# Sixteen instead of twenty-eight filling products of zeros on TensorE in the front of an attention and expert kernel

## The chip, the cores and the metric

The kernel runs on one core of a Trainium2 chip. The metric is the device time of one execution in microseconds (us); lower is better. A core has five engines that run side by side: PE (TensorE, whose loading of the stationary operand is shown apart as PEld), DVE (VectorE), ACT (ScalarE), POOL (GpSimd) and SP (SyncE, which here issues the DMAs).

## The reference, cut to what matters

A windowed attention with block summaries, for 4 batches of 8 heads, 768 positions and 64 features a head, and behind it a gated two-layer network on the 4 x 768 x 512 result.

```
scores_l = scale * q @ k.T           # kept where |i - j| < 16
scores_s = scale * q @ k_sum.T       # k_sum: maximum of each 32 keys; + log(32)
a = softmax([scores_l masked, scores_s])
x = a @ [v, v_sum]                   # v_sum: mean of each 32 values
xk, xr = mixes of x with x one position earlier (mu_k, mu_r)
out = sigmoid(xr @ w_r) * ((max(xk @ w_k, 0))**2 @ w_v)
```

## The kernel before, in words

A head pair fills the 128 partitions, so a batch has four sets (pairs), and each set is worked in two halves of 384 positions, which the code calls units. A unit is a row of steps on different engines: 24 small score products (L559, PE, into the banks `sc`), masking with a running minimum (L585, DVE), the exponential (L589, ACT), the inverse of the sums (L595 and L596, DVE), the scaling (L601, POOL), and for the first batch a transpose on PE (L608) whose result ACT copies out (L614); then 24 value products (L656). Before the first score of a set, DVE takes block maxima of the keys (L466 to L474) and copies them into the key tile `kt` (L478). For the first batch PE makes the block means of the values (L490, then L509 behind an ACT copy to the tile `sp` on L508); ACT copies them to `vm` (L511), and they are spread into the value tile `vx` (L515 or a DMA). The result of the attention goes to `vx` as well (L671), and is mixed (L682 on ACT or POOL, L688 on DVE) for the gate products (L730). The layers behind it are the products on L757 and L784, and for the last batch a seven-product scheme (L929, L1020). Weights come as 512 KB loads into three tiles `st`, are turned from 64-bit words into floats by ACT (L411) and DVE (L414, L416), and kept.

The order on every engine is fixed when the program is built: each step is an `op` with an engine, an assumed length and a due time, and `schedule()` places them one after the other by its own model of the engines, the DMA and the buffers. Steps without a buffer or with an unfinished input wait in lists; the earliest start wins, and among equals the earliest due time.

The front holds filling products too. `warm()` adds an op named "warm": one product of a 128 x 128 tile of zeros with itself (`zero_sb`, written once by POOL on L1066) into a free PSUM bank, which nothing reads. In the trace each shows as two matmul records and two weight loads of L440, so 28 of them are 56 records. `WARM` is how many are on offer. The planner takes one only where PE would otherwise stand idle for more than 300 ns by its own model and a bank is free, and none after a certain time or once the bank `pt` is given up:

```
    for _ in range(WARM):
        warm()
...
                if fill and (pick is None or pick[2] > fill[0] + GAP):
                    fill[1].place = spare[0][1]
                    pick = None, fill[1], fill[0]
```

With 260 on offer, 28 were taken, all in the first 20 us.

Of the kernel before, what the change touches and what calls it, by code (L numbers as in the profile page):

```python
# [65 lines left out]
PERIOD = 52000  # L66
STEP = 4800
SLACK = 400
WARM = 260
WARM_END = 110000  # L70
GAP = 300
COLD = 5000
# [236 lines left out]
def tile_kernel(ctx: ExitStack, tc: tile.TileContext, q, k, vT, v, consts, w_k, w_v, w_r, out):  # L309
# [129 lines left out]
    def warm():  # L439
        o = op("PE", "warm", 1.0e8, lambda: nc.tensor.matmul(  # L440
            o.place.tile(F32)[:, 512 - P:512], zero_sb, zero_sb, start=True, stop=True), reads=ZERO)
# [627 lines left out]
    for t in pools["y"]:  # L1069
        op("POOL", "tiny", None, lambda t=t: nc.gpsimd.memset(  # L1070
            t.tile(F32).rearrange("p (i c) -> p i c", c=P)[:, :, NK:P], 0.0))
    for _ in range(WARM):
        warm()
# [129 lines left out]
```

## Time and profile before

| what | before |
|---|---|
| median of 3 runs | 418.27 us (417.93 to 418.51) |
| the profiled execution, its own time | 418.56 us |
| its span, first to last instruction | 416.5 us |
| PE busy | 409.1 us (98%) |
| DVE, ACT, POOL busy | 344.8, 286.8, 125.9 us |
| records of L440 (filling products) | 56, between 1.0 and 20 us |

The span is 2.06 us shorter than the execution that it comes from. A row of the timeline gives the start in the span, the busy time of the merged stretch, engine, line, operation, tiles (written <- read), shapes and count; in brackets stands how long the engine was idle ahead of it, and what ended that. Matmul ends are modelled and take in the draining, so neighbouring rows overlap a little. The column PEclk is the granted TensorE clock as a share of full speed.

### The profile page before, as it was taken

To read this page: it belongs to the slowest core of one execution; us is meant where nothing else is said; L and a number is where in the kernel's file an instruction comes from. 1 tells how busy PE (TensorE), PEld (TensorE's weight loads), DVE (VectorE), ACT (ScalarE), POOL (GpSimd) and SP (SyncE) were. 2 spreads that over 40 slices of the span, in tenths; PEclk is the share of its full clock that TensorE was granted. 3 is DMA by queue.
4 is the path that set the end of the run, shared out by engine and by line. 5 is a ranking of instruction groups with operands and counts; after the bars stand their busy time and mean duration, and the time that the engine had idled before them with its cause. 6 is when DMAs were issued, how large, how long until landed. Compare 5 with 4: busy or idle time off the path is not lost.

```text
span 416.5 us, 9788 instructions
## 1 busy us (share of the span) xinstructions
PE 409.1 (98%) x3353; PEld 348.1 (84%) x3353; DVE 344.8 (83%) x1053; ACT 286.8 (69%) x815; POOL 125.9 (30%) x255
## 2 busy tenths in 40 slices
PE   8899999999999999999999999999999999999996
PEld 7654557788888888988888888988889899999996
DVE  3889999999998799889798778569386698878993
ACT  2889999899874599547674559466595675669710
POOL 0472565534660043502252000422433030104100
PEclk9999999999999999999999999999999999999999
DMA  8996679678878577777635454487855325230012
GB/s 295 407 296 216 222 257 318 235 251 235 240 210 264 173 248 196 230 267 247 215 120 159 158 183 172 133 297 200 252 150 143 103 75 146 59 113 15 0 59 94
DMA packets 48193, 79.68 MB, mean 191 GB/s; under 512 B 6736, under 2 KB 28176, under 8 KB 48144
## 3 DMA queue, kind: packets, MB, share of 16 engines
q1 hardware_dynamic: 48000, 78.78, 58.7%
q8 instruction: 26, 0.43, 0.4%
q10 hardware_dynamic: 144, 0.28, 0.3%
q14 instruction: 23, 0.19, 0.1%
HBM read 58.68 MB, written 20.07 MB: 189 GB/s over the span
## 4 chain that ended last, share of the span: by engine, by line
PE 83%; DMA 6%; DVE 5%; ACT 5%; issue 1%; SPq 1%; DVEq 0%; ACTq 0%
PE bank L784 24%; PE bank L757 23%; PE bank L929 14%; PE bank L656 5%; PE bank L1020 4%; PE bank L559 3%; PE bank L717 3%; PE bank L718 3%; PE bank L719 3%; DMA st<-in_w_r 2%; ACT y L589 2%; DMA st<-in_w_k 2%; DMA qt<-in_q 1%; DVE st L626 1%; DVE y L585 1%
## 5 line engine op out<-in xcount | busy, mean ns | idle before, releaser
L601 POOL TENSOR_SCALAR y<-y,rc 128x120 f32<-128x120 f32 x192 | 94.4, 510 | 130.5 <-DVE mn L585 49.2
L757 PE MATMUL bank<-xs,w 128*128 128x384 f32 x556 | 111.7, 349 | 0.0
L757 PEld LDWEIGHTS bank<-xs,w 128*128 128x128 f32 x556 | 98.1, 188 | 8.5 <-issue 1.0
L589 ACT ACTIVATE y<-y,mn 128x120 f32<-128x120 f32 x192 | 73.4, 384 | 15.3 <-DVE mn L585 15.1
L784 PE MATMUL bank<-w,kh 128*128 128x512 f32 x258 | 69.5, 397 | 0.4 <-DVE kh L770 0.4
L764 ACT ACTIVATE r<-bank 128x384 f32<-128x384 f32 x48 | 23.4, 488 | 51.0 <-PE bank L757 50.5
L784 PEld LDWEIGHTS bank<-w,kh 128*128 128x128 f32 x258 | 47.2, 188 | 9.4 <-DVE kh L770 0.7
L585 DVE CUSTOM_DVE_ANT_0 y<-bank,consts_sb 128x120 f32<-128x120 f32 x192 | 41.9, 273 | 0.1
L784 PE MATMUL bank<-w,kl 128*128 128x512 f32 x129 | 39.3, 397 | 0.0
L589 ACT ACTIVATION_READ_ACCUMULATOR y<-y,mn 128x1 f32 x192 | 36.2, 189 | 0.0
L656 PEld LDWEIGHTS bank<-pts,vx 120*64 120x64 f32 x768 | 24.0, 138 | 8.3 <-issue 7.1
L929 PE MATMUL bank<-xs,w 128*128 128x384 f32 x126 | 30.8, 337 | 0.0
L626 DVE STREAM_TRANSPOSE st<-y 128x384 f32<-128x384 f32 x48 | 27.1, 567 | 3.4 <-POOL y L601 2.8
L770 DVE CAST kh<-r 128x384 fp32r<-128x384 f32 x26 | 9.6, 370 | 23.0 <-ACT r L766 23.0
L784 PEld LDWEIGHTS bank<-w,kl 128*128 128x128 f32 x129 | 23.7, 188 | 5.6 <-issue 0.2
L685 POOL TENSOR_SCALAR xa<-vx,om_sb 128x384 f32<-128x384 f32 x11 | 8.7, 793 | 60.4 <-DVE xs L699 60.4
L656 PE MATMUL bank<-pts,vx 120*64 120x64 f32 x768 | 26.8, 224 | 0.0
L559 PEld LDWEIGHTS bank<-kt,qt 64*64 64x64 f32 x768 | 20.1, 133 | 7.9 <-issue 3.4
L559 PE MATMUL bank<-kt,qt 64*64 64x120 f32 x768 | 24.9, 268 | 1.7 <-DVE kt L478 1.1
L772 DVE TENSOR_TENSOR kl<-r,kh 128x384 fp32r<-128x384 f32 x43 | 24.1, 559 | 2.7 <-ACT kh L771 1.1
L766 ACT ACTIVATE r<-r 128x384 f32<-128x384 f32 x48 | 25.2, 525 | 0.7
L717 PE MATMUL bank<-w,xs 128*128 128x512 f32 x60 | 23.7, 395 | 0.0
(374 smaller groups left out, 824.2 us busy)
## 6 DMA issues: line engine op xcount, KB each, us to landing
vx<-in_v SPq DMA_DIRECT2D x32, 384.0 KB
far<-st SPq DMA_DIRECT2D x96, 96.0 KB
pts<-far SPq DMA_DIRECT2D x24, 384.0 KB
kt<-in_k SPq DMA_DIRECT2D x15, 544.0 KB
qt<-in_q SPq DMA_DIRECT2D x32, 192.0 KB
st<-in_vT SPq DMA_DIRECT2D x12, 384.0 KB
out<-z SPq DMA_DIRECT2D x18, 256.0 KB
st<-in_w_k SPq DMA_DIRECT2D x8, 512.0 KB
```

The lines of the kernel that those rows point to most:

```text
L559: nc.tensor.matmul(cells(to[h])[cs, i, 0:NK], t.t[hs, n * QW:(n + 1) * QW], kt.t[hs, w * KB:w * KB + NK], start=True, stop=True)
L585: op("DVE", "mask", None, lambda h=h, i=i, var=var: nc.vector.tensor_tensor_reduce(out=cells(y[h])[:, i, 0:NK], in0=cells(spot[h])[:, i, 0 ...
L589: op("ACT", "exp", None, lambda h=h, i=i: nc.scalar.activation(cells(y[h])[:, i, 0:NK], cells(y[h])[:, i, 0:NK], AF.Exp, bias=mn[h].t[:, i ...
L601: op("POOL", "norm", None, lambda h=h, i=i: nc.gpsimd.tensor_scalar(out=cells(y[h])[:, i, 0:NK], in0=cells(y[h])[:, i, 0:NK], scalar1=rc.t ...
L626: op("DVE", "flip", due - (FIRST_AHEAD if b == 1 else AHEAD) + 8000 + 600 * h, lambda h=h: nc.vector.transpose(out=turned()[:, :, h], in_= ...
L656: nc.tensor.matmul(av.t[hs, w * QW:(w + 1) * QW], windows(vw)[:, w, hs], weights_of(pts)[0:NK, 2 * c:2 * c + 2, h, i], start=True, stop=True)
L717: nc.tensor.matmul(ps.t, xh.t[:, ts], h, start=(p == 0), stop=False)
L757: nc.tensor.matmul(ps.t[:, 0:HT], w.t[:, p * P:(p + 1) * P], x[p][s].t, start=(n == 0), stop=(n == len(terms) * NPAIR - 1))
L766: op("ACT", "square", None, lambda: nc.scalar.activation(r.t, r.t, AF.Square), reads=[(r, 0)], writes=[(r, 0)])
L772: op("DVE", "sub", None, lambda: nc.vector.tensor_tensor(out=kl.t, in0=r.t, in1=kh.t.bitcast(F32), op=ALU.subtract), reads=[(r, 0), (kh, 0 ...
L784: nc.tensor.matmul(acc[t].t, a.t[:, t * P:(t + 1) * P], v.bitcast(F32) if single else v, start=start, stop=stop)
L929: nc.tensor.matmul(bank.t[:, 0:HT], pair[w].t[:, col:col + P], a[k][s].t, start=(first and n == 0), stop=(n == 3 * nk - 1), skip_group_che ...
```

## The change

One constant: the number of filling products on offer.

```
-WARM = 260
+WARM = 16
```

The planner takes all sixteen, at the first places where the old one took fillers, and has none left for the later places. The first place, eleven fillers ahead of the first score, is as before. The next place is PE between the first and the second set's scores (L559; `kt`, `qt` are keys and queries, `bank` a PSUM bank; the `x` at the end counts products, a filler being one). This is the difference there:

```order
 L559 MATMUL bank_0_158<-kt_0_110,qt_0_124 64x120 x2
 L559 MATMUL bank_0_161<-kt_0_110,qt_0_124 64x120 x2
-L440 MATMUL bank_0_122<-zero_sb 128x128 x10
+L440 MATMUL bank_0_122<-zero_sb 128x128 x5
 L559 MATMUL bank_0_158<-kt_0_127,qt_0_131 64x120 x2
 L559 MATMUL bank_0_161<-kt_0_127,qt_0_131 64x120 x2
```

Ten fillers have become five; nothing else stands elsewhere.

Then PE makes the first set's block means (L490), the second product on them (L509), the first transpose (L608) and the third set's scores (L559). The order before:

```order
L490 MATMUL bank_0_223<-vx_0_137,consts_sb 32x128 x2
L440 MATMUL bank_0_122<-zero_sb 128x128 x3
L509 MATMUL bank_0_255<-sp_70,consts_sb 24x128
L608 MATMUL bank_0_122<-consts_sb,y_0_113 120x128 x3
L440 MATMUL bank_0_267<-zero_sb 128x128 x3
L559 MATMUL bank_0_158<-kt_0_144,qt_0_149 64x120 x2
```

And the order now:

```order
L490 MATMUL bank_0_218<-vx_0_137,consts_sb 32x128 x2
L509 MATMUL bank_0_247<-sp_70,consts_sb 24x128
L608 MATMUL bank_0_122<-consts_sb,y_0_113 120x128 x3
L559 MATMUL bank_0_158<-kt_0_144,qt_0_149 64x120 x2
L559 MATMUL bank_0_161<-kt_0_144,qt_0_149 64x120 x2
```

The two groups of three fillers are gone, and the real products follow each other in the same order (the last number of a name is a running count, which shifts with fewer fillers; the banks are the same). One more filler, behind the fourth set's scores, is gone too. The other engines' rows, and PE's apart from L440, are the same in both programs from first to last.

## The prediction

> **What bounds the kernel now.** I read the page's shares first, then the span cut at 47.2 us, then the chain that ended last in its first part, then PE's own timeline around the fillers.
>
> ```profile
> PE 409.1 (98%) x3353; PEld 348.1 (84%) x3353; DVE 344.8 (83%) x1053; ACT 286.8 (69%) x815; POOL 125.9 (30%) x255
> ...
> PE 83%; DMA 6%; DVE 5%; ACT 5%; issue 1%; SPq 1%; DVEq 0%; ACTq 0%
> ```
>
> PE is busy 98% of the span and carries 83% of the chain. That share is an average over two stages. The windows' columns are stretch, length, PE busy with its count, clock, DMA share and GB/s:
>
> ```profile
> 0.00:47.20 47.20, 43.41 (x468) 1.00 0.83 295
> 47.20:416.50 369.30, 365.64 (x2886) 1.00 0.56 178
> ```
>
> Behind 47.2 us PE works 365.64 of 369.30 us: that stage is PE's own, the change has no instruction in it, and whatever the front gives or loses arrives there as a plain shift. In the front PE is busy too, but with fillers in that figure. Who sets the end of the front is told by the chain (start, length, what):
>
> ```profile
> 2.58 5.92 DMA qt<-in_q
> ...
> 8.52 9.51 DMA st<-in_w_r
> ...
> 18.05 0.67 ACT wc L411
> ...
> 22.55 0.59 ACT wc L411
> ...
> 23.16 6.57 DMA st<-in_w_k
> ...
> 47.19 2.84 PE bank L784 x6
> ```
>
> The front is loads and ACT, later DVE; the first PE piece on the chain is at 47.19. Until 18.05 the chain lies in transfers that the fillers don't touch. So a fill can matter only if a real product behind it starts late and that delay reaches ACT behind 18 us, or through the clock.
>
> **The change part by part.** PE's order is the same but for twelve fillers, 24 records. The timeline of PE around them:
>
> ```profile
> 0.99 4.72 PE L440 MATMUL bank<-zero_sb 128*128 128x128 f32 x22 [0.99 <-POOL zero_sb L1066]
> 6.48 0.85 PE L559 MATMUL bank<-kt,qt 64*64 64x120 f32 x24 [0.78 <-DVE kt L478]
> 7.26 2.50 PE L440 MATMUL bank<-zero_sb 128*128 128x128 f32 x20
> 10.02 0.42 PE L559 MATMUL bank<-kt,qt 64*64 64x120 f32 x4 [0.26 <-DVE mn L585]
> ...
> 11.39 0.86 PE L490 MATMUL bank<-vx,consts_sb 120*32 120x128 f32 x24
> 12.18 0.94 PE L440 MATMUL bank<-zero_sb 128*128 128x128 f32 x6
> 13.05 0.40 PE L509 MATMUL bank<-sp,consts_sb 128*24 128x128 f32 x2
> 13.38 0.54 PE L608 MATMUL bank<-consts_sb,y 128*120 128x128 f32 x3
> 13.76 0.83 PE L440 MATMUL bank<-zero_sb 128*128 128x128 f32 x6
> 14.71 0.85 PE L559 MATMUL bank<-kt,qt 64*64 64x120 f32 x24
> ...
> 18.79 0.85 PE L559 MATMUL bank<-kt,qt 64*64 64x120 f32 x24 [0.31 <-DVE kt L478]
> 19.56 0.49 PE L440 MATMUL bank<-zero_sb 128*128 128x128 f32 x2
> 20.66 0.51 PE L608 MATMUL bank<-consts_sb,y 128*120 128x128 f32 x3 [0.61 <-ACT pts L614]
> ```
>
> Directly taken off PE are 24 records. By the group of twenty, 2.50/20 = 0.125 us each, that is 3.0 us of PE time, and the question is what each stretch had hidden behind.
>
> Fillers 12 to 21 (7.26 to 9.76): the second set's scores still waited 0.26 us more for DVE's masks at 10.02. Five fewer end at 7.26 + 10 x 0.125 = 8.51, and PE then stands idle for 1.51 us. Gain 0.
>
> Fillers 22 to 24 (12.18): L509 starts right behind them at 13.05, so it might have waited for them. What it needs is ACT's copy to `sp`. The next rows show that, its reader on ACT, and DVE's key copy for the scores at 14.71:
>
> ```profile
> 12.68 0.24 ACT L508 COPY sp<-bank 128x128 f32<-128x128 f32 x1
> ...
> 13.72 0.26 ACT L511 COPY vm<-bank 24x128 f32<-24x128 f32 x1
> ...
> 18.05 0.67 ACT L411 ACTIVATE wc<-st 128x512 f32<-128x512 f32 x1 [0.19 <-DMA st<-in_w_r]
> ...
> 6.12 0.31 DVE L478 COPY kt<-ks 128x288 f32<-128x288 f32 x1
> ...
> 14.36 0.30 DVE L478 COPY kt<-ks 128x288 f32<-128x288 f32 x1
> ...
> 20.03 0.48 ACT L614 COPY pts<-bank 120x384 f32<-120x384 f32 x1
> ```
>
> `sp` is done at 12.92, 0.13 us ahead of L509. The same handoff from ACT to PE where no filler stands between, `pts` done at 20.51 and L608 at 20.66, took 0.15 us. So the filler cost L509 nothing that can be seen; its upper bound is 0.13 us. Even that would end at ACT, which waited 0.19 us for the w_r load at 18.05 in any case. Gain on the path 0, between 0 and 0.13.
>
> Fillers 25 to 27 (13.76): the scores at 14.71 start 0.05 us behind the end of the key copy, 14.66; the first set's scores at 6.48 also started 0.05 us behind their key copy's end at 6.43, without a filler ahead. Gain 0.
>
> Filler 28 (19.56): L608 at 20.66 waited 0.61 us for `pts` afterwards. Gain 0.
>
> Nothing reads the fillers' banks, no DMA or other engine's instruction goes with them, and no queue is passed, so no other term arises. The sum by instructions is 0, with -0.13 as its far end.
>
> **The term that isn't instructions: the clock.** The clock column says 1.00 from the first microsecond on, but the durations of one and the same filler don't (duration is minimum/median/maximum in ns; the first stretch is 2.6 to 4.4 us, the second 8 to 9):
>
> ```profile
> L440 PE MATMUL bank<-zero_sb x11: 421/421/421, 2.2 to 4.4; 128*128 128x128 f32 x11
> ...
> L440 PE MATMUL bank<-zero_sb x11: 275/275/275, 7.8 to 8.9; 128*128 128x128 f32 x11
> ```
>
> The first eleven fillers, 4.72/22 = 0.215 us a record, run slow; those behind the first scores fast. PE speeds up after some microseconds of work, and all eleven that stand ahead of the first score stay. What goes is the work that might keep it fast. How thin does it get? PE busy in stretches of 3.4 us, all of PE, then L440 alone, and then the end of the kernel:
>
> ```profile
> 8.60:12.00 3.40, 2.95 (x59) 1.00 1.03 409
> 12.00:15.40 3.40, 3.27 (x53) 1.00 1.03 408
> 15.40:18.80 3.40, 3.09 (x67) 1.00 1.04 406
> 18.80:22.20 3.40, 2.79 (x54) 1.00 1.02 403
> ...
> 8.60:12.00 3.40, 1.16 (x11) 1.00 1.03 409
> 12.00:15.40 3.40, 1.77 (x12) 1.00 1.03 408
> ...
> 411.40:414.80 3.40, 1.80 (x11) 1.00 0.25 92
> 414.80:416.50 1.70, 0.00 (x0) 1.00 0.24 89
> ```
>
> In 12.0 to 15.4 the fillers were 1.77 of 3.27 us; without them 1.50 of 3.40 us is left, 44%. In 8.6 to 12.0 it is 2.95 - 1.16 = 1.79, 53%. Before, the thinnest of these stretches was 82% (2.79 of 3.40). At the end a stretch of 53% (1.80) is followed by a clock still at 1.00, which is weak evidence, since the column missed the slow start as well. The longest idle piece would be the 1.51 us behind the five fillers, against 0.78 us before (5.7 to 6.48), after which the scores still ran 24 products in 0.85 us, as they did at 18.79.
>
> [...] I take 0 for the clock, because the front keeps 44% of work in its thinnest stretch and no gap is long; the other end is the first rival's price.
>
> The sum is 0 us against the profiled execution: span 416.5 us and 2.06 us around it, 418.56 us, which lies 0.29 us above the median of 418.27. Forecast for the median: 418.3 us. 0.2%, about what can be told from no change here, is 0.84 us.
>
> **Rivals.** First, slower: PE falls back to the pace of the first fillers in the thinned front. Price: slow against fast is 0.215/0.125 = 1.72. If 12.0 to 15.4 is too thin, the next 3.4 us run slow: PE's 3.09 us there become 5.3, 2.2 us more, of which the idle 0.31 us ahead of 18.79 and 0.61 us ahead of 20.66 take back 0.9. The 1.3 us left delay L608 and its copy, which ACT has in order ahead of the weight piece at 22.55 on the chain, and so the w_k load: about 418.3 + 1.3 = 419.6 us, 420.5 if nothing is taken back. It decides once about 2.4 us of PE work there run slow (0.84 + 0.9 = 1.75, over 0.72). For it: the share of work nearly halves. Against it: no long gap, and the 53% stretch at the end. [...] Chance 0.12.
>
> Second, faster: the fillers did hold up L509 and L608, and the freed queue passes it on. The bound is 0.13 us, 418.1 us; to be seen at all it would have to grow sixfold, for which no row speaks, so most of this case lies within 0.2% as well. A chance of 0.06 is for a real gain of over 0.84 us by something the rows don't show, such as a gain in the order of ACT's or the loads' work behind 18 us.
>
> Third, the faster pace comes late because eleven fillers aren't enough in some executions, so that the later ones mattered for it. Then the five others run slow, 10 x 0.215 = 2.2 us, from 7.26 to 9.4, still ahead of 10.02, where ten would have run to 11.6 and delayed the scores by 1.5 us. The loss is 0 and it lies with the forecast: 418.3 us.
>
> **Numbers.** Forecast with the third rival and the bounded part of the second, within 0.2%: 0.82. Faster by over 0.2%: 0.06. Slower by over 0.2%: 0.12. The range starts from the spread of the three runs, 0.58 us to either side of 418.27, adds 0.13 us below (417.6) and above about 0.25 us for a stretch that is slow in part only (419.1). The full price of the first rival lies outside.
>
> **What would show it.** Right: L440 with 32 records, the last near 8.5 us; idle stretches of about 1.5 us ahead of 10.02, 0.8 us ahead of 13.05 and 14.71, and 1.0 us ahead of 20.66, with those starts unmoved within 0.1 us; score groups still 0.85 us; the w_r load's end near 18.0 and the first L784 near 47.2. Wrong: products behind 10 us with durations like the first fillers (score groups well over 0.85 us, L490 over 0.86), a start that moves up by more than the 0.13 us allowed, or the chain entering PE's stage more than 0.8 us off 47.19.

## The result: 0.6% slower, and the profile after

The changed kernel took 420.41 us (median of 9 executions, 419.10 to 424.86) against 418.51 us for the kernel before beside it. The ratio is 1.0059, with a 95% interval of 1.0037 to 1.0082: 2.5 us by the ratio, outside the forecast range, on the first rival's side. The executions also spread over 5.8 us, where those of before spread over 1.4.

The profiled execution of the changed kernel took 424.86 us, span 423.0, so it is the slowest of the nine. From its page, PE's busy share and the clock in 40 slices:

```profile
PE 410.6 (97%) x3329; PEld 347.9 (82%) x3329; DVE 344.6 (81%) x1053; ACT 287.3 (68%) x815; POOL 126.1 (30%) x255
...
PEclk9699899999999999999999999999999999999999
```

There are 24 matmul records and 24 weight loads fewer, as said. New is the clock row: 6 in the second slice, 8 in the fifth. PE's timeline in the front (columns as before):

```profile
0.99 4.94 PE L440 MATMUL bank<-zero_sb 128*128 128x128 f32 x22 [0.99 <-POOL zero_sb L1066]
6.34 0.85 PE L559 MATMUL bank<-kt,qt 64*64 64x120 f32 x24 [0.41 <-DVE kt L478]
7.11 1.38 PE L440 MATMUL bank<-zero_sb 128*128 128x128 f32 x10
9.74 0.42 PE L559 MATMUL bank<-kt,qt 64*64 64x120 f32 x4 [1.24 <-DVE mn L585]
...
12.70 0.62 PE L509 MATMUL bank<-sp,consts_sb 128*24 128x128 f32 x2 [0.73 <-ACT sp L508]
...
14.44 1.48 PE L559 MATMUL bank<-kt,qt 64*64 64x120 f32 x24 [0.30 <-DVE kt L478]
...
16.68 1.51 PE L490 MATMUL bank<-vx,consts_sb 120*32 120x128 f32 x24
18.12 1.45 PE L656 MATMUL bank<-pts,vx 120*64 120x64 f32 x24
...
20.30 0.85 PE L559 MATMUL bank<-kt,qt 64*64 64x120 f32 x24
```

Up to 12.7 all is much as forecast: the idle pieces are 1.24 us (1.51 was forecast) and 0.73 us, and the starts lie 0.1 to 0.35 us earlier, as DVE's and ACT's steps ahead of them do (the first score at 6.34 for 6.48). Then the third set's 24 scores take 1.48 us in place of 0.85, the block means 1.51 in place of 0.86. The windows say why (stretch, length, PE busy with its count, granted clock, DMA share, GB/s):

```profile
5.70:9.10 3.40, 2.39 (x36) 1.00 1.00 378
9.10:12.50 3.40, 2.05 (x48) 1.00 1.03 412
12.50:15.90 3.40, 2.90 (x30) 0.50 1.03 401
15.90:19.30 3.40, 3.40 (x53) 0.50 1.04 414
...
43.20:46.60 3.40, 1.47 (x27) 1.00 0.38 142
46.60:50.00 3.40, 3.01 (x5) 0.50 0.78 263
```

After two stretches with PE 70% and 60% busy, the granted clock is half for 6.8 us, and half again behind the stretch with 43%. The fourth set's scores start at 20.30 in place of 18.79: 1.5 us late, by the clock.

That isn't all. Products on L730 at 33 us had won 0.65 of it back (33.98 for 33.12), and yet the first L784 came at 51.50 in place of 47.19. SP's queue shows the next loss, before and then after (start, length of the issue):

```profile
32.48 0.47 SPq L410 DMA_DIRECT2D st<-in_w_v  x1
33.00 0.41 SPq L548 DMA_DIRECT2D qt<-in_q  x1
33.52 0.37 SPq L410 DMA_DIRECT2D st<-in_w_k  x1
```

```profile
33.31 1.34 SPq L410 DMA_DIRECT2D st<-in_w_v  x1
34.71 0.41 SPq L548 DMA_DIRECT2D qt<-in_q  x1
35.23 0.37 SPq L410 DMA_DIRECT2D st<-in_w_k  x1
```

One issue takes 0.9 us longer, and the w_k load goes out 1.71 us later than before. ACT waits 2.30 us for it, and PE 2.32 us for ACT (kernel after, ACT's and PE's timeline):

```profile
42.24 0.67 ACT L411 ACTIVATE wc<-st 128x512 f32<-128x512 f32 x1 [2.30 <-DMA st<-in_w_k]
```

```profile
46.99 4.34 PE L757 MATMUL bank<-xs,w 128*128 128x384 f32 x8 [2.32 <-ACT r L764]
```

The 2.32 us are part of the stretch with 43%, behind which the clock fell a second time, so these eight products take 4.34 us in place of 2.85. Late by 0.76 us before the wait (the scores ahead of it start at 43.82 for 43.06), by 2.32 through it and by 1.5 through the second fall, less 0.3 won back, PE enters its stage 4.3 us late. The stage itself, from the first L784 to the end of the span, takes 371.5 us in place of 369.3: another 2.2 us, at a clock of 1.00, in a part of the program that has no filler at all.

What stands beside the long issue is one packet of the queue that carries instructions. Its rows in the DMA view, of before in 30 to 31.2 us and of after in 33.2 to 33.5 us (packets, MB, share of the engines):

```profile
q8 instruction: 1, 0.02, 5.0%
```

```profile
q8 instruction: 1, 0.02, 21.0%
```

This queue moves 26 packets of 16 KB in either kernel, one for about 258 of PE's instructions before (6706 matmuls and weight loads over 26) and 256 after (6658 over 26). So I take it to feed PE's instruction stream; its third packet also comes at 31.6 us or later in all traces with a shorter stream, and at 31.2 us or earlier in all others. With 48 instructions fewer, the third packet comes at 33.3 in place of 30.1 us, just when SP's long issue starts.

### The profile page after: what moved, and what is told of

It reads as the page before. It is cut to its first block, busy times and chain, and to the rows that moved or that the text cites. A ratio compares the mean times of both kernels' runs of the same rounds, so it can differ in the third digit from the quotient of the medians.

```text
span 423.0 us, 9740 instructions
## 1 busy us (share of the span) xinstructions
PE 410.6 (97%) x3329; PEld 347.9 (82%) x3329; DVE 344.6 (81%) x1053; ACT 287.3 (68%) x815; POOL 126.1 (30%) x255
## 4 chain that ended last, share of the span: by engine, by line
PE 78%; DVE 7%; DMA 6%; ACT 6%; issue 1%; SPq 0%; DVEq 0%; ACTq 0%
PE bank L757 22%; PE bank L784 21%; PE bank L929 14%; PE bank L656 5%; PE bank L1020 4%; PE bank L559 4%; DMA kt<-in_k 4%; ACT y L589 3%; PE bank L717 2%; PE bank L718 2%; PE bank L719 2%; DMA st<-in_w_k 2%; PE bank L608 1%; DVE y L585 1%; DVE st L626 1%
## 5 line engine op out<-in xcount | busy, mean ns | idle before, releaser
L757 PE MATMUL bank<-xs,w 128*128 128x384 f32 x556 | 113.4, 352 | 2.8 <-ACT r L764 2.3
L784 PE MATMUL bank<-w,kh 128*128 128x512 f32 x258 | 69.5, 397 | 0.4 <-DVE kh L770 0.4
L784 PEld LDWEIGHTS bank<-w,kh 128*128 128x128 f32 x258 | 47.2, 188 | 9.4 <-DVE kh L770 0.7
L784 PE MATMUL bank<-w,kl 128*128 128x512 f32 x129 | 39.4, 398 | 0.7 <-DVE kl L772 0.7
L929 PE MATMUL bank<-xs,w 128*128 128x384 f32 x126 | 30.8, 337 | 0.0
L784 PEld LDWEIGHTS bank<-w,kl 128*128 128x128 f32 x129 | 23.8, 188 | 6.7 <-DVE kl L772 1.1
L559 PEld LDWEIGHTS bank<-kt,qt 64*64 64x64 f32 x768 | 20.6, 135 | 8.6 <-issue 4.5
L559 PE MATMUL bank<-kt,qt 64*64 64x120 f32 x768 | 25.5, 273 | 2.1 <-DVE mn L585 1.4
L697 ACT CAST xs<-xa 128x384 fp32r<-128x384 f32 x40 | 20.0, 510 | 7.7 <-DVE xa L688 7.6
```

The costliest lines, as they stand in the source:

```text
L559: nc.tensor.matmul(cells(to[h])[cs, i, 0:NK], t.t[hs, n * QW:(n + 1) * QW], kt.t[hs, w * KB:w * KB + NK], start=True, stop=True)
L757: nc.tensor.matmul(ps.t[:, 0:HT], w.t[:, p * P:(p + 1) * P], x[p][s].t, start=(n == 0), stop=(n == len(terms) * NPAIR - 1))
L784: nc.tensor.matmul(acc[t].t, a.t[:, t * P:(t + 1) * P], v.bitcast(F32) if single else v, start=start, stop=stop)
L929: nc.tensor.matmul(bank.t[:, 0:HT], pair[w].t[:, col:col + P], a[k][s].t, start=(first and n == 0), stop=(n == 3 * nk - 1), skip_group_che ...
```

## The experiments

All ratios are against the kernel before on the same chip; each kernel had twelve executions, unless another number is given.

**How many fillers, and where.** Two kernels took other caps, a third left five fillers out of the full plan by their number:

```
-WARM = 260
+WARM = 21          # first kernel; 11 in the third
...
+            if not 17 <= n <= 21:       # second kernel, n counts the fillers emitted
```

> The first 21 fillers (11 and 10) stay, the last seven are gone. Theory A, the clock: the changed kernel's PE runs at half pace in stretches whose work got too thin; here only 12.0 to 15.4 and the place behind 19.5 us are thin, so the fall comes less often or later than in the changed kernel: median 418.6 to 420, mean granted clock below 1.000 in some executions at most. Theory B, a fixed price for each idle place (products behind a pause start late), independent of the clock: the loss of 1.9 us goes with the places emptied, three of four, so 419.5 to 420.2, with a narrow spread of 0.6 us.

> Fillers 17 to 21 alone are left out (the second place has five instead of ten); the last seven stay. Theory A: between 8.5 and 10 us PE idles, but the stretch behind it is full again; a fall of the clock needs a longer thin stretch, so 418.3 to 419.3 with the clock at 1.000 in most executions. Theory B: one of four places emptied, a quarter of the loss: 419.0, narrow.

> Only the eleven fillers ahead of the first score. Theory A: work is thinner still from 7.2 to 10 us, the clock falls earlier or rises later and in more executions: 421 to 424, spread of several us, mean clock 0.98 to 0.995 in most executions. Theory B: all four places emptied, one of them a little longer: 420.4 to 420.7, spread as before the change.

Measured: 21 fillers 421.61 us, ratio 1.0056 (1.0031 to 1.0081); without the five of the second place 420.63, 1.0031 (1.0012 to 1.0050); eleven fillers 422.21 (six executions), 1.0059 (1.0042 to 1.0075). The ratios grow neither with the places emptied nor with the stretch that is thin: emptying the last three places cost as much as the change itself, five fillers fewer in one place cost half of it. So theory A's and theory B's times were missed in the first two kernels; with eleven fillers theory A's time and clock were met (all six executions have a mean of 0.986 to 0.992), its wide spread wasn't (0.84 us). In all three traces the clock fell, at 20.9, 12.1 and 10.1 us. But in the first kernel five of twelve executions had a mean clock of 0.999 or 1.000 and still took 419.90 to 424.20 us. Neither theory gives that.

**The fillers' array work against their place in the queue.** The last twelve of 28 fillers are 8 columns wide:

```
+            w = P if n <= 16 else 8
+            nc.tensor.matmul(o.place.tile(F32)[0:w, 512 - w:512], zero_sb[:, 0:w], zero_sb[:, 0:w], start=True, stop=True)
```

> All 28 fillers stand where they stood before the change, but the last twelve are 8 columns wide in both operands instead of 128, so they take PE's queue and almost none of its array. Theory A: the clock follows the work in the array, so this is like the changed kernel: median 419.5 to 422, wide spread, clock below 1.000 in some executions. Theory B, with the price in pauses of the instruction stream or in PE's waking up: the products stand in a row as before, 418.3 to 418.9.

Measured: 419.23 us, 1.0000 (0.9981 to 1.0018). The clock's mean was 0.992 to 0.996 in five of twelve executions, PE was about as idle as in the changed kernel, and on the whole no loss can be told. A fall does cost time here too (those five have a median of 420.13 us, the other seven 418.98), but without a fall this kernel isn't slower than before. So theory A fails as the only cause. Theory B's pauses are there too (PE busy 2.15 us of 12.0 to 15.4, where 3.27 had been), so it fails as well. Four single executions gave more traces:

> The changed kernel once more, for a second trace. Theory A (the clock): the delay of the entry into PE's stage (first L784, 47.2 before the change) equals what slow products cost ahead of it; if no product behind the first score is slow, the entry is within 0.5 us of 47.2. Theory B (a fixed price of pauses): the entry is late by 0.6 us or more with all products fast.

> As the look before it, a third trace: theory A, an entry late by as much as slow products cost; theory B, late by 0.6 us or more without slow products.

> The kernel with all 28 fillers, the last twelve 8 columns wide, once more. Its mean clock was 0.992 in four of twelve executions, with little time lost. Theory A: if the clock falls in this one, it falls where PE has slack (before 12 us, or a stretch whose slow products end before their readers are free), and the entry is late by under 0.5 us. Theory B: no price, wherever the clock falls.

> As the look before it: theory A, a fall of the clock in a place with slack or none; theory B, no price wherever it falls.

The changed kernel took 422.01 and 422.12 us, its clock halved from 14.7 for 3.4 us and from 10.8 for 6.8 us; the kernel with thin fillers 419.29 (clock late to rise, at 10.3 us) and 419.79 us. In its second trace the clock falls much as in the changed kernel's:

```profile
8.60:12.00 3.40, 1.98 (x46) 0.93 1.04 411
12.00:15.40 3.40, 3.13 (x48) 0.50 1.02 403
15.40:18.80 3.40, 3.40 (x58) 0.57 1.04 403
```

Its fourth scores start at 20.16 us, those of the changed kernel's at 19.67 and 19.97. Yet its first L784 stands at 48.07, theirs at 48.74 and 48.66: from the L730 products at 33 us to there, the changed kernel's executions lost 1.3 and 0.7 us against the kernel before, this one 0.2. The fall cost this one 0.9 us at the entry, where theory A had allowed 0.5, and theory A has nothing for the rest. What the kernels differ in there is again SP: an issue of 1.00 and 1.52 us near 33.5 in the changed kernel, none over 0.5 among the w_v, qt and w_k issues with the thin fillers, whose PE stream is as long as before. That gave theory C, the length of the instruction stream.

**Clock and stream apart.** A helper `zeros(bank, rows, cols)` makes one product of zeros with `rows` columns of weights and `cols` moving columns. The first kernel has sixteen fillers, some wide; the second the changed kernel's sixteen and twelve tiny ones behind them:

```
+            cols = {12: 512, 13: 384, 14: 384, 22: 384, 25: 384}.get(n, P if n <= 11 else 0)
...
+            if n <= 16:
+                zeros(o.place, P, P)
+            if n == 16:
+                for _ in range(12):
+                    zeros(o.place, 8, 8)
```

> Sixteen fillers, so PE's instruction stream is as short as in the changed kernel, but five of them are 384 or 512 columns wide and stand in the second, third and fourth place (1280, 384 and 384 columns, as the 10, 3 and 3 fillers of 128 had), so PE is as busy as before the change. Theory A, the clock alone: like before, median within 0.4 us of the kernel before. Theory C, that the 48 instructions fewer move PE's instruction fetches (every 256 instructions; the third at 33.3 in place of 30.1 us), so that one meets SP's issue of the w_k load and holds it up by about 1 us: with the clock at 1.000 still 0.7 to 2 us slower than before, and an SP issue of over 0.9 us near 33 us with a fetch at the same time.

> The changed kernel, with 12 fillers of 8 columns added behind the five of the second place, so PE has as many instructions as before the change but its later places are empty. Theory A alone: the clock falls as in the changed kernel and the time with it, 420 to 422. Theory C alone: as before, within 0.4 us. Both: the clock falls in about half of the executions, which then lose 0.5 to 1 us; no SP issue of over 0.9 us near 33 us; median 0.2 to 0.8 us over before.

| | stream as before | 48 instructions shorter |
|---|---|---|
| places as full as before | 1 | 1.0041 (1.0018 to 1.0064), 420.65 us |
| places thin | 1.0018 (1.0003 to 1.0032), 419.74 us | the change: 1.0059 (1.0037 to 1.0082) |

The two parts add up to the whole: 0.41% and 0.18% are 0.59%, or 1.7 and 0.75 us. That the sum is exact is luck: each part is uncertain by 0.15 to 0.23%, and the kernel with thin fillers, which belongs into the same field as the tiny ones, had 1.0000. With the short stream and full places, nine of twelve executions kept a mean clock of 0.999 or 1.000, and their median is still 420.6 us against 418.83 before. With the long stream and thin places, the four executions at 0.999 or more took 418.90 to 419.39, the eight below 419.55 to 420.75: there a fall of the clock costs about 1.0 us (their medians are 419.07 and 420.07). The changed kernel's own four executions with a mean of 1.000 took 419.10 to 420.41 us, all above the median of before, 418.51: time is lost without a fall as well. SP's queue, first of the wide fillers with the packet of the instruction queue (32 to 34 us), then of the tiny ones:

```profile
32.00 0.47 SPq L410 DMA_DIRECT2D st<-in_w_v  x1
32.53 1.60 SPq L562 DMA_DIRECT2D qt<-in_q  x1
34.23 0.37 SPq L410 DMA_DIRECT2D st<-in_w_k  x1
```

```profile
q8 instruction: 1, 0.02, 3.9%
```

```profile
32.21 0.47 SPq L410 DMA_DIRECT2D st<-in_w_v  x1
32.74 0.41 SPq L564 DMA_DIRECT2D qt<-in_q  x1
33.25 0.37 SPq L410 DMA_DIRECT2D st<-in_w_k  x1
```

**Is it the length, or the form of the fillers?** Six kernels keep the places about as full and shift the stream, with wide fillers (fewer instructions) or halves of 64 by 64 (more); two more were made for the doubt that wide fillers cost something of their own.

```
+            cols = {12: 384, 13: 384, 14: 256, 15: 256}.get(n, 0 if 16 <= n <= 21 else P)   # -24
+            cols = {12: 256, 13: 256, 14: 0, 15: 0}.get(n, P)                               # -8
...
+            half = 12 <= n <= 27        # +64; 12 to 13: +8, 12 to 16: +20, 12 to 21: +40
+            for _ in range(2 if half else 1):
+                zeros(o.place, *((64, 64) if half else (P, P)))
```

> All places as busy as before, the second with four wide fillers of 1280 columns in all in place of ten: 24 PE instructions fewer. Theory A: as before, within 0.4 us. Theory C: the third fetch comes between 30.1 and 33.3 us; if it meets SP's issue of the spread or the w_v load at 31.6 to 32.9 us, a loss of 0.5 to 1.5 us, otherwise as before.

> All places as busy as before, the second with two fillers of 256 columns and six of 128: 8 PE instructions fewer. Theory A: as before. Theory C: the fetches hardly move, the third to about 30.4 us, still clear of the w_v and w_k issues: within 0.4 us of before, SP issues at 32 to 34 us under 0.5 us.

> The second place with two of its ten fillers split in halves: 8 PE instructions more. Theory A: as before. Theory C: third fetch near 29.7 us, clear of SP's issues: within 0.4 us of before.

> Five of the second place's ten fillers split: 20 PE instructions more. Theory A: as before. Theory C: third fetch near 29 us, close to SP's w_k issue at 29.0 us before: between as before and 1 us slower.

> All places as busy as before, but the second has 20 fillers of 64 by 64 in place of 10 of 128 by 128: 40 PE instructions more, so the fetches come 40 instructions earlier. Theory A: as before, within 0.4 us. Theory C: the time moves with the place that the fetches meet; the third fetch near 28 to 30 us, where SP's issues are those of the w_v and w_k loads of 27.1 and 29.0 us, so between 0.5 us faster and 1.5 slower than before.

> Sixteen fillers of the second to fourth place split: 64 PE instructions more. Theory A: as before. Theory C: third fetch near 27 us, close to the w_v issue at 27.05 us before; the front between as before and 1 us slower, and the later fetches all elsewhere, so 0.5 us faster to 2 us slower in all.

The two controls: the wide fillers of the first table with twelve tiny ones behind them (the same loop, behind filler 14), and the kernel before without the second place's last two fillers (`if n not in (20, 21)`).

> The sixteen fillers of which five are wide, with twelve of 8 columns added behind the second place's wide ones: PE as busy as before, its stream as long as before. Theory C (the length of the stream): as before, within 0.4 us, no SP issue of over 0.9 us near 33 us. Theory D (wide fillers cost something of their own): about as the kernel with the same wide fillers and the short stream, 1.2 to 2 us slower.

> The kernel before without the last two of the second place's ten fillers, which leaves PE idle for 0.25 us more there: 8 PE instructions fewer, no wide filler. Theory C: about as the kernel with 8 fewer through two wide ones, 0.5 to 1.2 us slower. Theory D: as before, within 0.4 us.

| instructions | fillers | median us | ratio (interval) | third fetch, us | longest issue of w_v, qt, w_k at 31 to 36 us |
|---|---|---|---|---|---|
| -48 | wide | 420.65 | 1.0041 (1.0018 to 1.0064) | 32.5 | 1.60 |
| -24 | wide | 420.68 | 1.0042 (1.0018 to 1.0066) | 32.1 | 1.12 |
| -8 | wide | 419.91 | 1.0027 (1.0010 to 1.0045) | 33.7 | 0.47 |
| -8 | two left out | 419.86 | 1.0012 (0.9998 to 1.0025) | 31.6 | 0.73 |
| 0 | wide, tiny | 419.27 | 1.0005 (0.9990 to 1.0020) | 29.6 | 0.47 |
| +8 | halves | 419.39 | 1.0004 (0.9993 to 1.0016) | 31.2 | 0.47 |
| +20 | halves | 419.38 | 1.0006 (0.9995 to 1.0017) | 29.0 | 0.47 |
| +40 | halves | 419.84 | 1.0019 (1.0004 to 1.0033) | 28.1 | 0.47 |
| +64 | halves | 419.51 | 1.0007 (0.9997 to 1.0017) | 28.5 | 0.47 |

Theory D is out: the same wide fillers cost 0.41% with the short stream and nothing that can be told with the old length. Halves as such cost nothing that can be told either (+8, +20, +64); so the 0.19% of +40, whose twelve executions all have a mean of 0.999 or more, is hardly theirs. It lies within what theory C allowed, though no issue near 33 us is held there. Theory C's detail held in part. The third fetch came about 1.5 us later than expected for +8 and +64. The issue at 31 to 36 us is held up in those traces whose third fetch comes at 32.1 to 33.6 us (the first two rows, the changed kernel's three, and the one with 21 fillers, 28 instructions shorter), a little (0.73 us) with the fetch at 31.6, and in none where it comes earlier. It isn't held either without the five fillers of the second place (fetch at 31.9) or with eleven fillers (38.9). The trace of -8 with wide fillers isn't a fair one for its front: its first score started at 7.86 us, with the clock rising at 13.7. Its expectation, within 0.4 us, was missed (0.86 us by the medians); the other kernel with -8 is 0.50 us slower by the medians, at the lower edge of theory C's range, with an interval that takes in 1, and settles nothing. None of the kernels is faster than the one before.

The clock isn't tied to these fillers alone. Of the kernel with wide fillers and the old length, whose places are as full as before, five of twelve executions have a mean of 0.995 or 0.996 and took 0.9 us longer (medians 419.71 and 418.77); of the kernel before, 6 of the 122 that ran beside the experiments are under 0.997. No trace of such an execution was kept.

**Left open.** The held issue near 33 us is one meeting of many: PE's stage lost more later. PE busy in 138 to 146 and 154 to 162 us, first of before, then of the wide sixteen, then of these with the stream filled up:

```profile
138.00:146.00 8.00, 8.00 (x118) 1.00 0.37 129
...
154.00:162.00 8.00, 8.00 (x83) 1.00 0.36 86
```

```profile
138.00:146.00 8.00, 7.32 (x79) 1.00 0.54 185
...
154.00:162.00 8.00, 7.52 (x81) 1.00 0.59 199
```

```profile
138.00:146.00 8.00, 8.00 (x118) 1.00 0.38 133
...
154.00:162.00 8.00, 8.00 (x83) 1.00 0.34 84
```

In that execution the front lost 0.35 us (first L784 at 47.54), although an issue of 1.60 us stood in it, and these two stretches 1.2 us of PE's time; some 0.7 us more show as no idle time. So in these traces more of the short stream's price lies in PE's stage than near 33 us: from the first L784 to the end the changed kernel's three traces took 371.2 to 371.7 us and the wide sixteen's 371.2, before 369.3, and all traces with a stream as long as before or longer 369.3 to 370.5. PE waits at 144 us for DVE, which had waited for a transfer that SP issues (the chain that ended last and PE's timeline, wide sixteen):

```profile
137.13 3.81 DMA farw<-wc
...
143.36 0.55 DVE kl L786
```

```profile
143.96 0.50 PE L798 MATMUL bank<-w,kl 128*128 128x512 f32 x1 [0.68 <-DVE kl L786]
```

SP has long issues at 138 to 165 us beside fetches in every trace, before included (1.5 us at 146.6, fetch at 146.7), so which meeting costs what isn't shown. One stands out: in seven of the twenty traces, all of them with a shorter stream, an SP issue of `far<-st` or `farw<-wc` at 120 to 124 us took 1.4 to 1.9 us beside a fetch, and these seven have the longest stages (370.8 to 371.7 us; the other thirteen 369.3 to 370.8). This was found in the traces afterwards and not tried.

That a fetch and a held issue belong together is plain from their number: over the twenty traces 213 of the 519 SP issues that overlap a fetch took over 0.9 us, and 65 of the 6821 others; with the fetches' times put 5 us later, 9 long issues would overlap one. That the fetch is what holds the issue wasn't tried by moving a fetch alone.

## Why the prediction was wrong

- **The instructions' sum of 0** held as far as it went: no product started earlier for the missing fillers (L509 0.06 us behind the end of ACT's copy to `sp`, 0.13 before), and idle time took their place.
- **"No DMA or other engine's instruction goes with them, and no queue is passed, so no other term arises"** is the step that failed most. By what the traces show, the fillers' own instructions come by DMA: with 48 fewer, the third packet of q8 came at 33.3 in place of 30.1 us. 48 fewer, with the places full, cost 0.41%, 1.7 us; that this goes by PE's fetches meeting SP's issues is the reading that the traces support. No rival had it. The row that could have warned stood in the page, 26 packets of q8; I took them as fixed.
- **"Whatever the front gives or loses arrives there as a plain shift"** failed with it. PE's stage behind the first L784 took 2.2 us longer in the profiled execution, and 1.9 and 2.4 us longer in the two others with a trace, without an instruction changed in it.
- **"I take 0 for the clock"** failed too. The fall that the first rival described came in seven of eleven executions of the changed kernel (mean clock under 0.997), not in 0.12 of them. Its mechanism was right, a thin stretch and products at half pace behind it; its place wasn't: the products were to be slow from 15.4 on, and the clock fell at 12.5 in the profiled execution, behind about the stretch that I had at 53%, and at 14.7 and 10.8 in the two other traces. Its price, 1.3 us, was of the right size: 1.5 us at the fourth scores in the profiled execution, about 1.0 us between the executions of the kernel with tiny fillers, 0.18% or 0.75 us over all of that kernel's. No run of before shows the 3.4 us over which that rival let the products run slow; in the traces with a fall the clock stayed at 0.50 for 3.4 or 6.8 us, with eleven fillers for 10.2.
- **"Because the front keeps 44% of work in its thinnest stretch and no gap is long"** was the reason for that 0, with the 53% at the end as a sign that such a share is enough. In the front 60% wasn't enough: the clock fell at 12.5 us behind it. Nor did it take a long gap: the longest idle piece was 1.24 us ahead of that fall and 2.32 us ahead of the second, where before had none over 0.78 us between PE's first and last product. The clock's changes in all twenty traces lie on a grid of 3.41 us, whose place differs from trace to trace (12.50, 19.32, 46.63 and 50.04 us in the changed kernel's profiled execution). Cut on it, the eight windows ahead of 410 us behind which the clock fell had PE busy for 28% to 60%, and of all the others at full clock one had less than 60% (59.7%), the rest 60.3% and more; the two windows of the first thin-filler trace that had 63% and 69% were passed at 1.00. So I take it that the share of work in one such window counts here; whether a thin stretch fills one or is split over two differs from execution to execution, which would explain why four of the eleven kept their clock (no trace of such a one was kept). It isn't the whole rule: in the last 10 us windows of 47% to 53% weren't followed by a fall in three traces.
- **The second and third rivals**: no gain appeared. A late rise did occur (10.3 and 13.7 us in two other kernels' traces), so eleven fillers don't always do; the first of these lost 0.65 us at the entry, where I had said 0.

## What to carry to other kernels

Work that only fills can be what holds the clock; here it fell to 0.50 behind windows in which PE was 28% to 60% busy. Before cutting such work, add up PE's busy share in every stretch of 3.4 us (the grid of these traces), wherever it may begin, and count anything near 60% or below as a risk, long idle time or none (1.24 us at most ahead of the fall at 12.5). Count instructions as well as time: in the changed kernel, with 48 fewer in PE's stream, the third fetch came at 33.3 in place of 30.1 us and each of the 23 behind it 4.2 to 13.0 us later than before; 48 fewer with full places cost 0.41%, thin places with the old length 0.18%. Don't take a stage without a changed instruction for a plain shift before its length has been compared (371.5 us for 369.3 here). To tell such causes apart, change one and hold the other by wide or tiny fillers, and read the clock's mean of each execution beside its time.

## What the runs showed of the hardware

- The clock fell to 0.50 for 3.4 or 6.8 us at a time (10.2 with eleven fillers), behind windows of 3.41 us, on a grid that differs from trace to trace, in which PE was 28% to 60% busy; in the changed kernel's profiled execution at 12.5 us behind 60% and at 46.6 us behind 43%.
- Queue q8 moves 26 packets of 16 KB in either kernel, for 6706 instructions of PE before and 6658 after; that they bring PE's instruction stream is my reading. That an issue on SP takes 1.0 to 1.6 us in place of 0.41 to 0.47 beside such a packet, I had not expected; of the issues beside a packet 41% took over 0.9 us, of the others 1%.
